# A fused attention and feed-forward kernel: score halves in separate banks, dummies at fixed places, one read moved, a new order for the first batch

## The chip, the cores and the metric

The kernel runs on one core of a Trainium2 chip. The metric is device time in microseconds (us); less is better. Five engines matter: PE (TensorE: matmuls, with its weight loads shown as PEld), DVE (VectorE), ACT (ScalarE), POOL (GpSimd) and SP (SyncE, which here issues most DMA transfers). Each engine works through its own list in order, and engines wait for each other through semaphores. SBUF is the working memory, PSUM the matmul output memory with eight banks of 128 x 512 float32, HBM the main memory.

## The reference

A two-way attention between tokens and a small state, for 8 batches with 8 heads, 512 tokens, 32 states and head width 64, then a two-layer network over all 8 x 544 rows:

```python
scores = x @ state.T / sqrt(D)          # per batch and head, 512 x 32
xread  = softmax(scores, over states) @ state
sread  = softmax(scores.T, over tokens) @ x
y = concat([xread, sread], rows)        # rows of all heads side by side: 4352 x 512
h = y @ w_in                            # 512 x 2048, given as float64
g = where(h >= 1, h, where(h <= -1, 0, (h + 1) ** 2 / 4))
out = g @ w_out                         # 2048 x 512, given as float64
```

## The kernel before

Stages run by batch (`b` = 0 to 7), and the 8 x 32 state rows come last as a ninth stage of half length. A batch has eight steps `j`, one for each 256 of the 2048 hidden columns.

The first attention product and the first layer are folded together: instead of `xread @ w_in` the kernel forms `sw` = state times the chunk of `w_in` (`sw_product`, L374), and the hidden block is `h` = softmax weights times `sw` (`Hidden.product`, L437). To keep float32 accuracy with a fast matmul format, operands are split into a high and a low part (`ath`/`atl`, `swh`/`swl`, `gh`/`gl`, `woh`/`wol`), and a product is three matmuls (L451 to L453 and L527 to L529). The activation is `relu` and `square` on ACT and `bound` on DVE; then `gh` (`high`, L480) and `gl` (`low`, L487). `g2` (L505) adds the output product, 24 matmuls of 512 columns for a step; it runs one step behind.

The weights arrive as float64 and are made float32 on the chip: `fetch` (L558) reads 1 MB per chunk, `low` (L564) and `high` (L577) convert the two halves of each number, `join` (L583) puts them together. On the orders below these are `dma.i.c`, `low.i.c`, `high.i.c`, `w.c` for chunk c of `w_in`, and `dma.o.c`, `low.o.c`, `high.o.c`, `join.c`, `woh.c`, `wol.c` for `w_out`. The tile for a chunk of `w_in` has two buffers, so the third chunk's read waits for the first chunk's join.

Batch 0 has all of this at once: weights, scores, softmax and products. Its order on each engine is written out in `SEQ` (L22 to L27), and `Plan` (L31) only works out from planned costs in which order the steps are emitted, and, in `emit` (L88), how many short dummy matmuls (`warm`, L162) fill the planned gaps on PE. Steps of the attention are `sc` (scores), `turn` (transposition of the scores), `top1`, `less1`, `exp1`, `sum1`, `inv1`, `norm1`, `back` (softmax over states); `park` (L285) copies batch 0's scores aside for the later softmax over tokens (`top2`, `exp2`, `turn_blocks`, `shuffle`), whose weighted sum is `read2` (L327) with `scale2` and `place2` behind it. Batch 0's scores come in two halves (`sc.0.0`, `sc.0.1`), both written into one tile of two banks (`ps_mm`, one buffer). Other PSUM tiles are `ps_acc` (four banks) and `ps_h` (two banks). Engines that touch the same tile's bank take turns.

From batch 1 on the order is that of the loop at L870. At step 0 of a batch, between the two halves of the last output product, stand `read2` of that batch, four groups of `sw` products and the next batch's scores; `later` (L814) hangs further steps of the attention at the middle (`mid`) or end of a step. Batch 0's second softmax is hung in batch 1 (L852 to L854), its `read2` stands behind that of batch 2 (L880), and the `place2` of batches 0, 1 and 2 together at step 1 of batch 2 (L848). `place2` issues 16 small transfers on SP, `shuffle` 16 as well.

Of the kernel before, what the change touches and what calls it, by code (L numbers as in the profile page):

```python
# [104 lines left out]
def state_exchange_moe(  # L105
# [56 lines left out]
    def warm(n):  # L162

        for _ in range(n):
            nc.tensor.matmul(warmed[:, :P], lhsT=ident, rhs=ident, start=True, stop=True)  # L165
# [37 lines left out]
    class Attention:  # L203
# [9 lines left out]
        def scores(self, half=None):  # L213
            b = self.b
            if half != 1:
                sc = self.both = ps_mm(f"sc{b}")
# [4 lines left out]
            for pr in range(NPR):
                for hh in range(2):
                    rows = slice(hh * 64, hh * 64 + 64)
                    o = self.sc[hh][pr * NS:(pr + 1) * NS]
# [3 lines left out]
                    nc.tensor.matmul(o, lhsT=sb[rows, b, pr], rhs=m, start=True, stop=True)  # L228

# [3 lines left out]
        def turn(self, q, half=None):  # L233
            t = self.tokens(half)
            nc.vector.transpose(out=self.z[:, q, t], in_=self.sc[q][:, t])  # L235
# [49 lines left out]
        def park(self):  # L285
            self.e2 = srT.rearrange("p a b n -> p (a b n)").rearrange("p (q t) -> p q t", q=2)
            nc.scalar.copy(out=self.e2, in_=self.both)
            self.seen = [self.e2[:, q] for q in range(2)]

        def top2(self, q):  # L290
            b = self.b
# [7 lines left out]
            nc.vector.tensor_reduce(out=nm, in_=self.seen[q], op=ALU.max, axis=AX.X, negate=True)  # L299
            nc.vector.tensor_scalar_mul(nm, nm, SCALE)  # L300

        def exp2(self, q):
            nc.scalar.activation(
                out=self.e2[:, q], in_=self.seen[q], func=AF.Exp, bias=self.nm2[:, q:q + 1],
                scale=SCALE, accum_out=self.sum2[:, q:q + 1],
# [258 lines left out]
    def low(kind, c, engine):  # L564
# [7 lines left out]
        else:  # L572
            nc.scalar.activation(
                out=lo, in_=lo.bitcast(U32), func=AF.Relu, scale=0.875 * 2.0 ** -29, bias=offset
# [369 lines left out]
```

## Time and profile before

| | us |
|---|---|
| median of 3 runs | 643.0 |
| lowest and highest | 642.75, 643.68 |
| profiled execution | 644.25 |
| its span, first to last instruction | 642.4 |
| 512-column matmul, from start to start | 0.227 |
| DVE STREAM_TRANSPOSE of 128x512 (L275), ACT COPY of the scores (L287) | 0.68, 1.01 |

The page lists busy time of each engine and groups of instructions, the timeline lists single instructions with the wait ahead of them in brackets and what ended it, and busy time can be asked for any stretch. A timeline row reads: start, duration, engine, line, operation, output and inputs, shape, count, and in brackets the idle time before it with its releaser. A row of a stretch reads: its length, then busy time and number of instructions (x) of PE, PEld, DVE, ACT and POOL, then the granted clock, the share of the DMA engines and GB/s. A matmul's own duration is longer than the distance between two, since they overlap. A row of a waits view reads: total, times, longest.

### The profile page before, as it was taken

How to read it: one execution, taken by the hardware profiler on the slowest of the kernel's cores; microseconds unless marked ns; L12 is line 12 of the kernel's file. 1: busy time of each engine (PE TensorE's matmuls, PEld its weight loads, DVE VectorE, ACT ScalarE, POOL GpSimd, SP SyncE). 2: the span in 40 equal slices, each digit the busy share in tenths (PEclk: the TensorE clock that was granted, in tenths of full speed). 3: DMA queues.
4: the chain of work that ended last, by engine and by line, in shares of the span. 5: the costliest groups of instructions: out<-in, count | busy, mean ns of one | idle time of the engine just before them, and what ended most of it. 6: DMA issues, size and time to landing. Idle time of an engine off the chain costs nothing.

```text
span 642.4 us, 10553 instructions
## 1 busy us (share of the span) xinstructions
PE 630.6 (98%) x4348; PEld 512.7 (80%) x4348; DVE 361.0 (56%) x539; ACT 370.7 (58%) x536; POOL 0.8 (0%) x7
## 2 busy tenths in 40 slices
PE   6999999999999999999999999999999999999997
PEld 5677787888788887888788887888788878888896
DVE  5999966555455536654565536653565534335431
ACT  5999865565555555555655556555755555444641
POOL 0000000000000000000000000000000000000000
PEclk9999999999999999999999999999999999999999
DMA  7996033123303301121212212011202110000101
GB/s 313 383 407 240 1 62 104 66 34 44 124 7 82 87 25 52 62 34 65 69 68 30 69 53 85 9 26 65 71 2 33 66 67 5 1 0 1 66 1 33
DMA packets 52191, 48.40 MB, mean 75 GB/s; under 512 B 42288, under 2 KB 42416, under 8 KB 49200
## 3 DMA queue, kind: packets, MB, share of 16 engines
q1 hardware_dynamic: 51808, 47.40, 22.9%
q8 instruction: 34, 0.56, 0.4%
q10 hardware_dynamic: 336, 0.33, 0.2%
q14 instruction: 13, 0.11, 0.1%
HBM read 34.08 MB, written 8.91 MB: 67 GB/s over the span
## 4 chain that ended last, share of the span: by engine, by line
PE 92%; DVE 4%; ACT 2%; DMA 1%; issue 1%; POOL 0%; ACTq 0%; POOLq 0%
PE acc L528 18%; PE acc L529 18%; PE acc L527 18%; PE h L451 10%; PE h L452 10%; PE h L453 10%; PE sw L386 4%; PE sr L337 1%; PE sc L228 1%; DMA raw_i<-in_moe_w_in_dram 1%; ACT raw_i L581 1%; DVE w L593 1%; PE warmed L165 1%; DVE u L475 0%; DVE z L235 0%
## 5 line engine op out<-in xcount | busy, mean ns | idle before, releaser
L529 PE MATMUL acc<-wo,gl 128*128 128x512 f32 x544 | 211.9, 389 | 0.1
L528 PE MATMUL acc<-wo,gh 128*128 128x512 f32 x544 | 211.7, 389 | 0.0
L527 PE MATMUL acc<-wo,gh 128*128 128x512 f32 x544 | 211.7, 389 | 0.0
L468 ACT ACTIVATE u<-h,half 128x512 f32<-128x512 f32 x136 | 93.3, 690 | 168.0 <-PE h L453 165.4
L475 DVE SCALAR_TENSOR_TENSOR u<-u,h 128x512 f32<-128x512 f32 x136 | 92.7, 686 | 167.7 <-ACT u L472 167.6
L489 DVE TENSOR_TENSOR gl<-u,gh 128x1024 fp32r<-128x1024 f32 x68 | 83.3, 1225 | 74.8 <-ACT gh L626 74.6
L529 PEld LDWEIGHTS acc<-wo,gl 128*128 128x128 f32 x544 | 102.1, 188 | 21.9 <-DVE gl L489 0.8
L528 PEld LDWEIGHTS acc<-wo,gh 128*128 128x128 f32 x544 | 102.1, 188 | 21.1
L527 PEld LDWEIGHTS acc<-wo,gh 128*128 128x128 f32 x544 | 102.1, 188 | 21.1
L626 ACT CAST gh<-u 128x1024 fp32r<-128x1024 f32 x66 | 69.3, 1050 | 40.6 <-DVE u L475 40.3
L472 ACT ACTIVATE u<-u 128x512 f32<-128x512 f32 (+1 forms) x128 | 84.4, 660 | 4.1
L386 PE MATMUL sw<-w,sb 64*32 64x256 f32 x1024 | 34.1, 379 | 3.7 <-DVE w L593 3.1
L386 PEld LDWEIGHTS sw<-w,sb 64*32 64x32 f32 x1024 | 20.3, 106 | 14.5 <-DVE w L593 4.0
L542 ACT COPY o<-acc 128x512 f32<-128x512 f32 x33 | 19.1, 587 | 15.3 <-PE acc L529 15.3
L451 PE MATMUL h<-ath,sw_3h 128*128 128x512 f32 x64 | 25.3, 395 | 0.8 <-DVE u L475 0.8
L452 PE MATMUL h<-ath,sw_3l 128*128 128x512 f32 x64 | 24.9, 390 | 0.0
L453 PE MATMUL h<-atl,sw_3h 128*128 128x512 f32 x64 | 24.9, 389 | 0.0
L451 PE MATMUL h<-ath,sw_1h 128*128 128x512 f32 x60 | 24.3, 405 | 0.0
L452 PE MATMUL h<-ath,sw_1l 128*128 128x512 f32 x60 | 23.5, 391 | 0.0
L453 PE MATMUL h<-atl,sw_1h 128*128 128x512 f32 x60 | 23.4, 390 | 0.0
L451 PE MATMUL h<-ath,sw_5hl 128*128 128x512 f32 x56 | 21.8, 389 | 0.0
L452 PE MATMUL h<-ath,sw_5hl 128*128 128x512 f32 x56 | 21.8, 389 | 0.0
(175 smaller groups left out, 715.0 us busy)
## 6 DMA issues: line engine op xcount, KB each, us to landing
xt<-in_xt_dram SPq DMA_DIRECT2D x16, 512.0 KB, 4.6
raw_i<-in_moe_w_in_dram SPq DMA_DIRECT2D x8, 1024.0 KB, 6.7
raw_o<-in_moe_w_out_dram SPq DMA_DIRECT2D x8, 1024.0 KB, 10.3
out_dram<-o SPq DMA_DIRECT2D x32, 256.0 KB, 2.1
xn<-in_x_dram SPq DMA_DIRECT2D x7, 1024.0 KB, 4.8
e<-eb SPq DMA_DIRECT2D x112, 32.0 KB, 2.0
srT<-rt SPq DMA_DIRECT2D x128, 4.0 KB, 1.7
xn<-in_x_dram SPq DMA_DIRECT2D x2, 512.0 KB, 4.5
```

What stands on the lines that cost most here:

```text
L386: nc.tensor.matmul(banks[hh][pr * NS:(pr + 1) * NS, i * CI:(i + 1) * CI], lhsT=sb[rows, bi, pr], rhs=w32[ci][rows, pr], start=True, stop=True,
L451: nc.tensor.matmul(o, lhsT=wh[:, k, sl], rhs=ah[:, k], start=first, stop=False)
L452: nc.tensor.matmul(o, lhsT=wl[:, k, sl], rhs=ah[:, k], start=False, stop=False)
L453: nc.tensor.matmul(o, lhsT=wh[:, k, sl], rhs=al[:, k], start=False, stop=last)
L468: nc.scalar.activation(out=self.u[:, i], in_=self.hs[i], func=AF.Relu, scale=0.5, bias=half)
L472: nc.scalar.activation(out=u, in_=u, func=AF.Square)
L475: nc.vector.scalar_tensor_tensor(out=self.u[:, i], in0=self.u[:, i], scalar=1.0, in1=self.hs[i], op0=ALU.min, op1=ALU.max,)
L489: nc.vector.tensor_tensor(out=gl, in0=self.u, in1=gh.bitcast(F32), op=ALU.subtract)
L527: nc.tensor.matmul(a, lhsT=lh, rhs=oh, start=f == 0, stop=False)
L528: nc.tensor.matmul(a, lhsT=lh, rhs=ol, start=False, stop=False)
L529: nc.tensor.matmul(a, lhsT=ll, rhs=oh, start=False, stop=f == NF - 1)
L626: nc.scalar.copy(out=out, in_=src)
```

## The change

Scores: the second half of batch 0's scores goes to two `ps_h` banks instead of the other columns of the first tile, and `park` becomes two steps of two copies each. Dummies: `warm` makes one matmul of 512 columns instead of 128; two at the start instead of seven, and four ahead of `sw.0.0` and one ahead of `p.0.0.0` by a table (`FILL`), none by planned gaps. Batch 0's second softmax moves to batch 1's step 1, and its `read2` and `scale2` to step 5, `place2` to step 6; batch 1's `place2` moves to step 4 of batch 2. Batch 7's last `sw` group takes the `ps_mm` tile instead of two `ps_acc` banks. The ACT form of `low` has another scale and no bias tile. The order lists of batch 0 change.

```diff
-WARM = 7
+WARM = 2
+FILL = {"sw.0.0": 4, "p.0.0.0": 1}
-            if self.engine[k] == "PE":
-                if begun[first] < begun[k] < begun[until]:
-                    n = int((begun[k] - idle) / 0.34)
-                    if n > 0:
-                        fill(n)
-                idle = done[k]
+            fill(FILL.get(k, 0))
             self.ops[k][2]()
...
-            nc.tensor.matmul(warmed[:, :P], lhsT=ident, rhs=ident, start=True, stop=True)
+            nc.tensor.matmul(
+                warmed.rearrange("p (a c) -> p a c", c=P), lhsT=ident, rhs=ident[:, None].broadcast_to([P, 4, P]),
+                start=True, stop=True,
+            )
...
-                sc = self.both = ps_mm(f"sc{b}")
-                self.sc = [sc[:, hh] for hh in range(2)]
+                sc = ps_mm(f"sc{b}")
+                self.sc = [[sc[:, hh]] for hh in range(2)]
...
+            else:
+                for hh in range(2):
+                    self.sc[hh].append(ps_h(f"sc{b}_{hh}"))
...
-        def park(self):
-            self.e2 = srT.rearrange("p a b n -> p (a b n)").rearrange("p (q t) -> p q t", q=2)
-            nc.scalar.copy(out=self.e2, in_=self.both)
-            self.seen = [self.e2[:, q] for q in range(2)]
+        def park(self, half):
+            if half == 0:
+                self.e2 = srT.rearrange("p a b n -> p (a b n)").rearrange("p (q t) -> p q t", q=2)
+            for q in range(2):
+                nc.scalar.copy(out=self.e2[:, q, self.tokens(half)], in_=self.seen(q, half))
...
-                out=lo, in_=lo.bitcast(U32), func=AF.Relu, scale=0.875 * 2.0 ** -29, bias=offset
+                out=lo, in_=lo.bitcast(U32), func=AF.Relu, scale=0.9375 * (2.0 ** -29 - 2.0 ** -49)
...
+    def one(b, *names):
+        for name in names:
+            f, *q = name.split()
+            getattr(atts[b], f)(*map(int, q))
+
+    later("mid", 1, 1, (one, 0, "top2 0", "exp2 0", "top2 1", "exp2 1"))
+    later("end", 1, 1, (one, 0, "turn_blocks 0", "turn_blocks 1", "shuffle"))
     later("end", 1, 2, (load_later, 0))
-    later("mid", 1, 4, *[(f, q) for q in range(2) for f in (lambda q: atts[0].top2(q), lambda q: atts[0].exp2(q))])
-    later("end", 1, 5, *[(lambda q: atts[0].turn_blocks(q), q) for q in range(2)], (lambda: atts[0].shuffle(),))
+    later("mid", 1, 5, (one, 0, "read2", "scale2"))
+    later("mid", 1, 6, (one, 0, "place2"))
+    later("mid", 2, 4, (one, 1, "place2"))
     for b in range(2, B):
-        later("mid", b, 1, (place_all, b))
+        later("mid", b, 1, (one, b, "place2"))
...
-                sr = atts[b].read2()
-                if b == 2:
-                    atts[0].read2(sr)
+                atts[b].read2()
...
-                sw_product([(b, 7), (b + 1, 0)][:B - b], ps_acc, "raw")
+                sw_product([(b, 7), (b + 1, 0)][:B - b], ps_acc if b + 1 < B else None, "raw")
```

The orders (`SEQ`) of batch 0 and the first steps of the next, broken into lines here, old (-) and new (+); a step is named with its batch and chunk or step, `p.i.0.j` is half i of hidden block j, `g2.i.0.j` half i of its output product:

```
-SP:
-    dma.xt.0.0 dma.xt.0.1 dma.i.0 dma.i.2 dma.o.0 dma.i.1 dma.o.1 dma.sb.1 dma.i.4 dma.i.3 dma.o.2 dma.xt.1
-    dma.o.4 dma.i.5 dma.i.6 dma.o.3 dma.o.5 dma.o.6 dma.xn.1 dma.i.7 dma.o.7 dma.xt.2 dma.eb.1
+SP:
+    dma.xt.0.0 dma.xt.0.1 dma.i.0 dma.i.2 dma.o.0 dma.i.1 dma.o.1 dma.o.2 dma.i.4 dma.i.3 dma.o.4 dma.o.3 dma.o.7
+    dma.sb.1 dma.i.5 dma.xt.1 dma.i.6 dma.o.6 dma.xt.2 dma.xn.1 dma.o.5 dma.i.7 dma.eb.1
-PE:
-    warm sc.0.0 sc.0.1 sw.0.0 p.0.0.0 p.1.0.0 sw.0.1 sw.0.2 p.0.0.1 p.1.0.1 g2.0.0.0 g2.1.0.0 p.0.0.2 sw.0.3
-    p.1.0.2 g2.1.0.1 sc.1 p.0.0.3 p.1.0.3 g2.0.0.1 g2.1.0.2 g2.0.0.2 p.0.0.4 sw.0.5 p.1.0.4 g2.0.0.3 g2.1.0.3
-    p.0.0.5 p.1.0.5 g2.1.0.4 sw.0.7 p.0.0.6 p.1.0.6 g2.1.0.5 g2.0.0.4 p.0.0.7 p.1.0.7 g2.0.0.5 g2.0.0.6 g2.1.0.6
+PE:
+    warm sc.0.0 sc.0.1 sw.0.0 p.0.0.0 p.1.0.0 sw.0.2 sw.0.1 p.0.0.1 p.1.0.1 g2.0.0.0 g2.1.0.0 p.0.0.2 sw.0.3
+    p.1.0.2 g2.1.0.1 g2.0.0.1 p.0.0.3 p.1.0.3 sc.1 g2.0.0.2 g2.1.0.2 p.0.0.4 p.1.0.4 g2.1.0.3 sw.0.5 g2.0.0.3
+    p.0.0.5 p.1.0.5 g2.0.0.4 g2.1.0.4 sw.0.7 p.0.0.6 p.1.0.6 g2.1.0.5 g2.0.0.5 p.0.0.7 p.1.0.7 g2.0.0.6 g2.1.0.6
-DVE:
-    turn.0.1.0 top1.0.1.0 turn.0.0.0 top1.0.0.0 turn.0.1.1 turn.0.0.1 top1.0.1.1 less1.0.1 top1.0.0.1 less1.0.0
-    w.0 sum1.0.0 inv1.0.0 sum1.0.1 norm1.0.0 inv1.0.1 back.0.0 norm1.0.1 back.0.1 w.2 ath.0.1 join.0 w.1 atl.0.1
-    atl.0.0 bound.1.0.0 swl.0.1 bound.0.0.0 wol.0 gl.0.0 low.o.1 low.i.3 swl.0.2 w.4 join.1 bound.0.0.1
-    bound.1.0.1 w.3 gh.0.1 wol.1 gl.0.1 swl.0.3 join.2 bound.0.0.2 woh.2 bound.1.0.2 wol.2 top2.1.0 turn.1.0
-    gl.0.2 low.i.5 top2.1.1 turn.1.1 w.5 w.6 join.3 top1.1.1 bound.0.0.3 bound.1.0.3 top1.1.0 wol.3 gl.0.3
...
+DVE:
+    turn.0.1.0 turn.0.0.0 turn.0.1.1 top1.0.1.0 turn.0.0.1 top1.0.0.0 top1.0.1.1 top1.0.0.1 less1.0.1 less1.0.0
+    w.0 sum1.0.0 sum1.0.1 inv1.0.0 norm1.0.0 inv1.0.1 back.0.0 norm1.0.1 back.0.1 w.2 low.i.1 atl.0.0 w.1 atl.0.1
+    join.0 bound.1.0.0 swl.0.1 bound.0.0.0 wol.0 gl.0.0 low.i.4 join.1 swl.0.2 w.4 low.i.3 bound.0.0.1 bound.1.0.1
+    w.3 wol.1 gl.0.1 join.2 low.o.7 swl.0.3 woh.2 wol.2 bound.1.0.2 bound.0.0.2 join.4 gl.0.2 join.3 turn.1.1
+    top2.1.0 woh.3 turn.1.0 bound.1.0.3 bound.0.0.3 top2.1.1 wol.3 top1.1.1 gl.0.3 w.6 w.5
...
-ACT:
-    park.0 low.i.0 high.i.0 exp1.0.0 low.i.2 exp1.0.1 high.i.2 swh.0.0 high.o.0 ath.0.0 low.o.0 high.i.1 low.i.1
-    relu.0.0.0 relu.1.0.0 square.0.0 swh.0.1 woh.0 swh.0.2 gh.0.0 high.i.4 low.i.4 relu.0.0.1 high.o.1 relu.1.0.1
-    square.0.1 high.i.3 low.o.2 woh.1 high.o.2 swh.0.3 relu.0.0.2 relu.1.0.2 square.0.2 low.o.4 high.i.5 low.i.6
-    gh.0.2 high.o.4 low.o.3 high.o.3 exp2.1.0 high.i.6 relu.0.0.3 relu.1.0.3 square.0.3 exp2.1.1 woh.3 high.o.5
-    gh.0.3 high.o.6 swh.0.5 relu.0.0.4 low.o.6 relu.1.0.4 square.0.4 woh.4 high.i.7 gh.0.4 low.i.7 exp1.1.0 woh.5
...
+ACT:
+    park.0.0 low.i.0 high.i.0 exp1.0.1 exp1.0.0 low.i.2 high.i.2 swh.0.0 park.0.1 low.o.0 ath.0.0 ath.0.1 high.i.1
+    high.o.0 relu.0.0.0 relu.1.0.0 square.0.0 swh.0.1 woh.0 swh.0.2 gh.0.0 high.o.1 low.o.1 high.i.4 relu.0.0.1
+    relu.1.0.1 square.0.1 high.i.3 woh.1 high.o.2 gh.0.1 low.o.2 relu.0.0.2 swh.0.3 relu.1.0.2 low.o.4 square.0.2
+    low.o.3 high.o.4 gh.0.2 high.o.3 low.i.5 high.i.5 relu.1.0.3 relu.0.0.3 square.0.3 low.i.6 exp2.1.0 low.o.6
+    gh.0.3 high.i.6 woh.4 relu.0.0.4 exp2.1.1 relu.1.0.4 square.0.4 high.o.7 swh.0.5 high.o.5 gh.0.4 low.o.5
+    high.i.7
...
```

More of the change, by code (lines that the diff above doesn't have):

```diff
@@ L86, in times, with emit @@
         self.begun, self.done = begun, done
-    def emit(self, fill, first, until):
+    def emit(self, fill):
         self.times()
-        begun, done = self.begun, self.done
-        idle = 0.0
         place = {k: i for seq in SEQ.values() for i, k in enumerate(seq.split())}
-        for k in sorted(begun, key=lambda k: (begun[k], place[k])):
-            if self.engine[k] == "PE":
-                if begun[first] < begun[k] < begun[until]:
-                    n = int((begun[k] - idle) / 0.34)
-                    if n > 0:
-                        fill(n)
-                idle = done[k]
+        for k in sorted(self.begun, key=lambda k: (self.begun[k], place[k])):
+            fill(FILL.get(k, 0))
             self.ops[k][2]()
@@ L157, in state_exchange_moe @@
     nc.vector.memset(half, 0.5)
-    offset = small.tile([P, 1], F32, name="offset")
-    nc.vector.memset(offset, 0.49)
     warmed = ps_acc("warmed")
@@ L223, in scores, with seen @@
                     rows = slice(hh * 64, hh * 64 + 64)
-                    o = self.sc[hh][pr * NS:(pr + 1) * NS]
+                    o = self.sc[hh][-1][pr * NS:(pr + 1) * NS]
                     m = self.xt[rows, :, pr]
                     if half is not None:
-                        o, m = o[:, half * S // 2:(half + 1) * S // 2], m[:, half]
+                        o, m = o[:, :S // 2], m[:, half]
                     nc.tensor.matmul(o, lhsT=sb[rows, b, pr], rhs=m, start=True, stop=True)
+        def seen(self, q, half=None):
+            return self.sc[q][0] if half is None else self.sc[q][half][:, :S // 2]
         def tokens(self, half):
@@ L233, in turn @@
         def turn(self, q, half=None):
-            t = self.tokens(half)
-            nc.vector.transpose(out=self.z[:, q, t], in_=self.sc[q][:, t])
+            nc.vector.transpose(out=self.z[:, q, self.tokens(half)], in_=self.seen(q, half))
         def parts(self, q):
@@ L298, in top2 @@
             nm = self.nm2[:, q:q + 1]
-            nc.vector.tensor_reduce(out=nm, in_=self.seen[q], op=ALU.max, axis=AX.X, negate=True)
+            src = self.seen(q) if b else self.e2[:, q]
+            nc.vector.tensor_reduce(out=nm, in_=src, op=ALU.max, axis=AX.X, negate=True)
             nc.vector.tensor_scalar_mul(nm, nm, SCALE)
@@ L303, in exp2 @@
             nc.scalar.activation(
[L304 to L305 removed]
+                out=self.e2[:, q], in_=self.seen(q) if self.b else self.e2[:, q], func=AF.Exp,
+                bias=self.nm2[:, q:q + 1], scale=SCALE, accum_out=self.sum2[:, q:q + 1],
             )
@@ L325, in shuffle, with read2 @@
                     )
-        def read2(self, sr=None):
+        def read2(self):
             b = self.b
             xn = loaded.pop(("xn", b))
-            c0 = 0 if sr is None else D
-            sr = ps_mm(f"sr{b}") if sr is None else sr
-            self.sr = sr[:, :, c0:c0 + D]
+            self.sr = ps_mm(f"sr{b}")[:, :, :D]
             for q in range(2):
@@ L340, in read2 @@
                         )
-            return sr
         def scale2(self):
@@ L675, in att_ops1 @@
                     h = k + (half,)
-                    op(("turn",) + h, "DVE", 0.35, m("turn", q, half), [("sc", b, half)], ends=[("sc", b)])
+                    op(("turn",) + h, "DVE", 0.35, m("turn", q, half), [("sc", b, half)],
+                       ends=[("sc", b, half), ("sch", b)][:1 + half])
                     op(("top1",) + h, "DVE", 0.35, m("top1", q, half), [("turn",) + h])
@@ L696, in att_ops2 @@
         if b == 0:
-            op(("park", b), "ACT", 0.95, m("park"), [("sc", b, 1)], ends=[("sc", b)])
+            for half in range(2):
+                op(("park", b, half), "ACT", 0.7, m("park", half), [("turn", b, q, half) for q in range(2)],
+                   ends=[("sc", b, half), ("sch", b)][:1 + half])
             return
@@ L702, in att_ops2 @@
             op(("top2",) + k, "DVE", 0.75, m("top2", q), [("sc", b)] + [("top2", b, 0)] * q, take=take)
-            op(("exp2",) + k, "ACT", 0.66, m("exp2", q), [("top2",) + k], ends=[("sc", b)])
+            op(("exp2",) + k, "ACT", 0.66, m("exp2", q), [("top2",) + k, ("turn",) + k], ends=[("sc", b)])
         for q in range(2):
@@ L788, in state_exchange_moe @@
         tensor(("sc", 0, side), 0.6, lambda side=side: att_start(0, side), [("dma", "xt", 0, side)],
-               take=[("mm", ("sc", 0))] * (1 - side), ends=[("xt", 0)])
+               take=[("mm", ("sc", 0, 0)), ("h", ("sc", 0, 1)), ("h", ("sch", 0))][side:1 + 2 * side], ends=[("xt", 0)])
     att_ops1(0)
@@ L884, in state_exchange_moe @@
                 sw_product([(b, 5), (b, 6)], ps_acc, "xn")
-                for c in (0, 2) if b == 2 else (b,):
-                    atts[c].scale2()
+                atts[b].scale2()
                 if b + 1 < B:
                     att_start(b + 1)
-                sw_product([(b, 7), (b + 1, 0)][:B - b], ps_acc, "raw")
+                sw_product([(b, 7), (b + 1, 0)][:B - b], ps_acc if b + 1 < B else None, "raw")
                 for c in (1, 3, 5, 7):
```

6 lines of the change are left out of this document (1 added, 5 removed), and 8 rows, old and new, of the table SEQ.

## The prediction

> **What bounds the kernel now.** First the busy times on the page, then busy time, clock and DMA by stretch (edges: the first matmul of batch 0's split products at 24.60 us, then the last matmul of each batch).
>
> ```profile
> PE 630.6 (98%) x4348; PEld 512.7 (80%) x4348; DVE 361.0 (56%) x539; ACT 370.7 (58%) x536; POOL 0.8 (0%) x7
> ```
>
> ```profile
> 0.00:24.60 24.60, 18.28 (x169) 13.42 (x169) 16.02 (x31) 16.72 (x22) 0.84 (x7) 1.00 0.83 326
> 24.60:96.67 72.07, 71.11 (x400) 55.04 (x400) 64.76 (x85) 61.71 (x74) 0.00 (x0) 1.00 0.54 203
> 96.67:168.32 71.65, 71.61 (x498) 57.98 (x496) 41.21 (x69) 40.69 (x64) 0.00 (x0) 1.00 0.28 74
> 168.32:241.42 73.10, 72.64 (x561) 58.93 (x560) 39.24 (x63) 39.41 (x60) 0.00 (x0) 1.00 0.20 54
> 241.42:312.43 71.01, 71.01 (x497) 57.85 (x496) 38.46 (x61) 39.32 (x60) 0.00 (x0) 1.00 0.19 54
> ```
>
> TensorE fills the span at a granted clock of 1.00, so only four places can give time: the start (24.6 us, whose real matmuls need about 7; 11.7 of its TensorE time are dummies), small waits in batch 0, and whatever batches 1, 2 and 7 have over a plain batch. A plain batch is 71.01; batch 1 has 0.64 more, batch 2 has 2.09 more. In batch 0 DVE and ACT are 90% and 86% busy, so there the order of their work counts.
>
> The start, by the timeline:
>
> ```profile
> 1.45 3.36 PE L165 MATMUL warmed<-ident 128*128 128x128 f32 x14 [1.45 <-POOL ident masks.py:199]
> 6.36 0.67 PE L228 MATMUL sc<-xt,sb 64*32 64x256 f32 x16 [0.62 <-DVE z L235]
> 6.96 3.62 PE L165 MATMUL warmed<-ident 128*128 128x128 f32 x30
> 8.52 1.25 ACT L573 ACTIVATE raw_i<-raw_i,offset 128x1024 int32<-128x1024 uint32 x1
> 8.66 0.78 DVE L235 STREAM_TRANSPOSE z<-sc 128x256 f32<-128x256 f32 x2 [0.62 <-ACT srT L287]
> 9.66 1.13 ACT L581 ACTIVATE raw_i<-raw_i 128x1024 f32<-128x1024 f32 x1
> 11.44 1.22 DVE L593 SCALAR_TENSOR_TENSOR w<-raw_i 128x1024 int32<-128x1024 int32 x1
> 12.69 0.33 SPq L561 DMA_DIRECT2D raw_i<-in_moe_w_in_dram  x1
> 12.71 0.67 PE L386 MATMUL sw<-w,sb 64*32 64x256 f32 x16 [2.14 <-DVE w L593]
> 16.26 3.67 PE L463 MATMUL h<-zt,sw_0w 128*128 128x512 f32 x8 [1.12 <-DVE zt L275]
> 19.08 1.19 ACT L581 ACTIVATE raw_i<-raw_i 128x1024 f32<-128x1024 f32 x1 [0.96 <-DMA raw_i<-in_moe_w_in_dram]
> 21.25 1.27 ACT L468 ACTIVATE u<-h,half 128x512 f32<-128x512 f32 x2
> 21.42 1.23 DVE L593 SCALAR_TENSOR_TENSOR w<-raw_i 128x1024 int32<-128x1024 int32 x1 [1.41 <-ACT raw_i L573]
> 26.88 1.23 DVE L489 TENSOR_TENSOR gl<-u,gh 128x1024 fp32r<-128x1024 f32 x1
> 28.16 0.50 PE L529 MATMUL acc<-wo,gl 128*128 128x512 f32 x1
> ```
>
> One chain: scores, softmax halves on DVE, chunk 0 joined (11.44), which frees the buffer for chunk 1's read (12.69, landed 18.99), chunk 1 split and joined (21.42), hidden block 0 on ACT and DVE, until its `gl` (26.88) lets the output product go on (28.16). The two waits of 0.62 are engines taking turns at one score tile.
>
> **The change part by part.**
>
> *Warm-up, 7 short dummies to 2 long.* 14 records in 3.36 are 0.24 each; the later ones, 30 in 3.62, are 0.12, so the first run at half rate. A 512-column record at full rate is 3.67/8 = 0.46, doubled and times 4: 3.4 to 3.7. I take nothing (bounds -0.1 and +0.3).
>
> *Second half of the scores in other banks, park in two.* Both 0.62 waits go. The next limit is chunk 0 itself, which landed at about 8.4:
>
> ```profile
> raw_i<-in_moe_w_in_dram SPq DMA_DIRECT2D x1, 1024.0 KB, 6.7
> raw_i<-in_moe_w_in_dram SPq DMA_DIRECT2D x1, 1024.0 KB, 6.3
> L568 DVE TENSOR_SCALAR raw_i<-raw_i x2: 686/689/692, 28.6 to 45.8; 128x1024 int32<-128x1024 uint32 x2
> ```
>
> (the issue at 1.68, the issue at 12.69, and the low word on DVE). DVE would be ready for the join at 10.3, but ACT's two passes end at 10.79 as before, so the join moves from 11.44 to 10.75: **-0.7**. Exps then follow at 10.65; the softmax steps keep their lengths, and `back` of both halves ends some 0.9 earlier, so the first products start near 15.3 for 16.26. The second park stands ahead of them, since its banks are theirs; it ends near 15.15 by the order on ACT: no wait, with 0.15 to spare.
>
> *Dummies before sw.0.0 and p.0.0.0.* 4 x 0.86 end near 10.1, 1 x 0.86 near 13.5: both in front of waits to 11.9 and 15.3. Nothing.
>
> *Chunk 1.* Its read moves 0.7 with the join; the same 6.3 gives 18.25. What is queued beside it is now o.2's 1 MB for sb's 448 KB (bounds 17.6 to 19.2). Its low word goes to DVE: 0.69 beside ACT's pass instead of after it, so its join stands at 19.5 for 21.42, and ACT, with two high passes left (2 x 1.04), reaches hidden block 0 at 20.4 for 21.25. DVE holds `atl` and the join of o.0 behind that landing; both are due only after 22. From there ACT's order is unchanged up to `gh` (relu, square, swh, woh, swh), so `gl` moves from 26.88 to 25.9 and the output product from 28.16 to 27.1: **-1.05**, bounds -1.8 and -0.2 with the landing.
>
> *The rest of batch 0's order.* ACT gets six steps from DVE and gives five: lows of o.1, i.5, o.5 (3 x 1.13 apart), two `gh` (0.95 each) and one `ath` (0.5) against four lows and one `woh`: +0.3 on ACT, -0.6 on DVE, so neither is relieved. What PE waits for now:
>
> ```profile
> 52.69 1.27 DVE L475 SCALAR_TENSOR_TENSOR u<-u,h 128x512 f32<-128x512 f32 x2
> 53.42 0.50 PE L451 MATMUL h<-ath,sw_3h 128*128 128x512 f32 x1 [0.82 <-DVE u L475]
> ```
>
> That is 1.2 between matmul starts, and 0.25 more in smaller waits. Followed step by step along the new lists with the durations above, chunk 3's join ends at 33.9 and holds sw.0.3 by 0.3; the bounds of block 2 end at 42.4, 0.5 late for block 3; the bounds of block 3, two low or high passes less in front of them on ACT, end before 51 and hold nothing; swl of chunk 5 costs 0.3. So 1.1 for 1.45: -0.35, batch 0 together **-1.4**. Bounds: all waits gone, -2.4; these three doubled and chunk 1 late, +0.5. On SP, xt.2 now waits for scores 1 (about 46), and i.7 for chunk 5's join (about 56.7), landing at 62 to 64; chunk 7 is wanted near 69.8: hidden by some 2 us.
>
> *Batch boundaries.*
>
> ```profile
> 98.02 3.22 PE L386 MATMUL sw<-w,sb 64*32 64x256 f32 x95
> 100.87 0.10 PEld L386 LDWEIGHTS sw<-w,sb 64*32 64x32 f32 x1 [0.52 <-issue]
> 168.63 1.10 PE L337 MATMUL sr<-xn,e 128*32 128x64 f32 x64
> 169.55 1.20 PE L337 MATMUL sr<-xn,srT 128*32 128x64 f32 x64
> 170.68 1.51 PE L386 MATMUL sw<-w,sb 64*32 64x256 f32 x43
> 172.64 1.22 PEld L386 LDWEIGHTS sw<-w,sb 64*32 64x32 f32 x51 [0.94 <-issue]
> 241.74 1.10 PE L337 MATMUL sr<-xn,e 128*32 128x64 f32 x64
> 242.77 2.82 PE L386 MATMUL sw<-w,sb 64*32 64x256 f32 x96
> 526.94 0.29 DVE L346 TENSOR_TENSOR rs<-sr,r 128x128 f32<-128x128 f32 x1 [0.99 <-PE sr L337]
> PEld sw L386 <- DVE sw_1l L413: 0.6, 2, 0.4
> L165 PE MATMUL warmed<-ident 128*128 128x128 f32 x80 | 11.7, 306 | 1.4 <-POOL ident masks.py:199 1.4
> q8 instruction: 34, 0.56, 0.4%
> ```
>
> Batch 2's 2.09 hold the second read (64 matmuls, 1.03) and 1.06 of idle put down to "issue". Moved into batch 1 the read costs 1.03 plus a change of shape on either side (241.74 to 242.77, and about 0.1 each): 1.25. Gain 0.85 if the idle goes. Queue q8 moved 34 packets for 2 x 4348 PE instructions: 256 each. I read the idle as PE outrunning such a packet: it comes where short matmuls use up 256 instructions fastest. An estimate from these rows, with 0.016 for a read (1.03/64), 0.029 for a sw (2.82/96): the 160 matmuls up to a packet's edge must last 4.2 to 4.6 us. Batch 1's edge at its 95th sw gives 0.23 + 64 x 0.016 + 95 x 0.029 = 4.0 (idle 0.6); batch 2's at its 43rd, 117 x 0.016 + 43 x 0.029 = 3.1 (idle 1.05); counting on, batches 3 to 6 have 4.8 or more, and none idles. The change drops 80 - 14 = 66 dummy records with their loads, half a packet: batch 1's edge falls among 0.23 us matmuls, **-0.6** (bounds -0.64 and +0.4). Batch 2's, counted on over 564 matmuls, then falls behind its sw: 51 x 0.016 + 96 x 0.029 + 13 x 0.054 (scores) = 4.3, idle 0.3 at most, which I take: **-0.5** (bounds -0.85 and +0.2). The Trainium skill ("Runtime: NRT & Kernel Launch", Instruction fetch mechanics) has the same 256 instructions in 16 KiB, but calls the refill mostly hidden; by that, the idle is something else and does not move with the count, which is a rival below.
>
> Batch 7's last chunk waits 0.6 for sw_1l to leave its banks; in the score tile, free once the read is scaled (526.94 + 0.29, two us earlier), it does not: **-0.5** (bounds -0.6, 0). The earlier steps of attention 0 (DVE 3.5 us in batch 1's step 1) lie in DVE's 42% of idle there; 16 DMAs instead of 48 at one place come off SP only.
>
> **Sum**: -1.4 - 0.6 - 0.5 - 0.5 = -3.0. The profiled execution took 644.25 (span 642.4): 641.25. The median of the runs is 643.0, and the same terms give **640.0**.
>
> **The rivals.**
>
> *The clock drops.* With fewer dummies TensorE works 1.3 of the 5 us between 18.75 and 23.8. For: the cold 0.24. Against: 2.14 idle at 12.71, at full rate after. If it drops, 12 matmuls take 0.43 for 0.23, 2.4 more, of which 0.5 lies in the wait for `gl`: +1.9, 641.9. The Trainium skill ("TensorE: Matmul & The Clock Gate", Why this matters for your kernels) wants no idle gap above about 3 us; no single gap here reaches that.
>
> *The idle at boundaries stays*, whatever the instruction count: batch 1 gives 0 and batch 2 costs +0.2: -1.4 - 0.5 + 0.2 = -1.7, 641.3. For: "issue" names no cause. Against: five batches without it.
>
> *Batch 0 gives nothing*: chunk 1's landing does not move, or the new lists wait on ACT twice as long as I find (its 86% speaks for that): -1.6, 641.4.
>
> *Slower: the edges land badly.* If my count is off by some 30 matmuls, packet edges sit in the reads of batches 3 to 7, where none idles now: 5 x 1.05 = +5.25 with -1.7 for the rest: 646.5. It turns slower once two of the five are hit at full price.
>
> **How the numbers follow.** Chances: forecast 0.55 (638.6 to 641.0), clock 0.12, idle stays 0.13, batch 0 nothing 0.14, edges 0.06. A measurement tells 0.2% (1.3 us) from none: faster means below 641.7. The forecast, both 641.3 cases for the most part and little of the clock's lie there: 0.81; same 0.13, slower 0.06. Range 638.6 to 641.9.
>
> **What would show it.** Right: second scores with no wait, chunk 0's join near 10.75, chunk 1's near 19.5, first `gl` product near 27.1; batch 1 about 72.3 (71.01 and the read), batch 2 about 71.3, no sw_1l wait in batch 7. Wrong: 512-column matmuls 0.43 apart after 23 us; "issue" at other boundaries; new waits on `u` or `w` between 33 and 62.

## The result and the profile after

| | us |
|---|---|
| before, median of 5 runs beside it | 643.68 (642.75 to 645.57) |
| after, median of 5 runs | 640.56 (640.12 to 641.01) |
| ratio, 95% interval | 0.9947 (0.9926 to 0.9968) |
| after, profiled execution and its span | 640.56, 638.8 |

The changed kernel is 3.1 us faster (643.68 - 640.56; 2.1 to 4.8 by the interval of the ratio), where 3.0 was forecast. The page of after, and its stretches by the same edges as before (first split product of batch 0 at 22.25, then the last 512-column matmul of each batch):

```profile
PE 627.1 (98%) x4282; PEld 505.7 (79%) x4282; DVE 359.6 (56%) x536; ACT 370.2 (58%) x539; POOL 0.8 (0%) x7
```

```profile
0.00:22.25 22.25, 15.23 (x102) 5.29 (x103) 15.66 (x30) 15.86 (x25) 0.83 (x7) 0.99 0.90 360
22.25:93.90 71.65, 71.65 (x400) 56.42 (x400) 63.90 (x84) 62.11 (x75) 0.00 (x0) 0.98 0.54 204
93.90:166.16 72.26, 72.26 (x562) 58.70 (x560) 41.86 (x71) 40.85 (x64) 0.00 (x0) 1.00 0.28 75
166.16:237.78 71.62, 71.62 (x497) 58.03 (x496) 38.52 (x61) 39.32 (x60) 0.00 (x0) 1.00 0.19 54
237.78:308.79 71.01, 71.01 (x497) 57.84 (x496) 38.45 (x61) 39.32 (x60) 0.00 (x0) 1.00 0.18 54
```

The end of batch 0 came from 96.67 to 93.90: -2.77, twice the forecast's -1.4. Batches 1 and 2 together took 143.88 (72.26 + 71.62) for 144.75 (71.65 + 73.10): -0.87, where -1.1 was forecast: batch 1 is as forecast (72.26, a plain batch and the read's 1.25), batch 2 kept 0.61 over a plain 71.01. The rest is equal to 0.01, batch 7 too. -2.77 - 0.87 is the span's -3.6; the medians differ by less, and the second profile of before, below, shows a likely reason.

The chain of the start in after, by the timeline:

```profile
5.89 0.67 PE L226 MATMUL sc<-xt,sb 64*32 64x256 f32 x16 [0.17 <-DMA xt<-in_xt_dram]
10.56 1.22 DVE L591 SCALAR_TENSOR_TENSOR w<-raw_i 128x1024 int32<-128x1024 int32 x1 [0.61 <-ACT raw_i L579]
11.81 0.33 SPq L559 DMA_DIRECT2D raw_i<-in_moe_w_in_dram  x1
15.16 3.67 PE L461 MATMUL h<-zt,sw_0w 128*128 128x512 f32 x8 [1.59 <-DVE zt L275]
16.91 1.20 ACT L579 ACTIVATE raw_i<-raw_i 128x1024 f32<-128x1024 f32 x1
18.55 1.22 DVE L591 SCALAR_TENSOR_TENSOR w<-raw_i 128x1024 int32<-128x1024 int32 x1
19.05 1.23 ACT L466 ACTIVATE u<-h,half 128x512 f32<-128x512 f32 x2
22.25 0.77 PE L449 MATMUL h<-ath,sw_1h 128*128 128x512 f32 x1 [1.76 <-DVE u L473]
24.53 1.22 DVE L487 TENSOR_TENSOR gl<-u,gh 128x1024 fp32r<-128x1024 f32 x1
26.99 0.39 PE L527 MATMUL acc<-wo,gl 128*128 128x512 f32 x1
170.76 0.10 PEld L226 LDWEIGHTS sc<-xt,sb 64*32 64x32 f32 x1 [0.49 <-issue]
526.90 0.50 PE L449 MATMUL h<-ath,sw_1h 128*128 128x512 f32 x1 [0.49 <-DVE sw_3l L411]
```

The waits of 0.62 on the score tile are gone, chunk 0 joins at 10.56 (forecast 10.75) and the first products start at 15.16 (15.3). Then chunk 1 runs ahead of the forecast: its read landed 5.0 after its issue, not 6.3, and its join is at 18.55, not 19.5. `gl` is ready 1.4 earlier than forecast, yet the first `gl` product starts at 26.99, almost the 27.1 of the forecast, because the clock fell in between (experiment 2 has the same order and no fall here, and starts it at 25.96):

```profile
20.00:22.00 2.00, 0.49 (x16) 0.01 (x2) 2.00 (x3) 1.97 (x5) 0.00 (x0) 0.99 1.02 418
22.00:24.00 2.00, 1.75 (x4) 1.55 (x5) 2.00 (x5) 1.88 (x3) 0.00 (x0) 0.50 0.98 414
24.00:26.00 2.00, 2.00 (x7) 1.52 (x7) 1.97 (x3) 2.00 (x3) 0.00 (x0) 0.65 1.05 438
```

The granted clock is the third number from the end. The last two rows of the chain belong to batches 2 and 7: 0.49 of "issue" idle stands behind the 13th of 16 scores, and the first hidden product of batch 7 waits for `sw_3l` where it used to wait for its chunk's turn.

### The profile page after: what moved, and what is told of

The parts are those of the page before. It is cut to its first block, busy times and chain, and to the rows that moved or that the text cites. A ratio compares the mean times of both kernels' runs of the same rounds, so it can differ in the third digit from the quotient of the medians.

```text
span 638.8 us, 10423 instructions
## 1 busy us (share of the span) xinstructions
PE 627.1 (98%) x4282; PEld 505.7 (79%) x4282; DVE 359.6 (56%) x536; ACT 370.2 (58%) x539; POOL 0.8 (0%) x7
## 4 chain that ended last, share of the span: by engine, by line
PE 95%; ACT 1%; DVE 1%; DMA 1%; issue 0%; SPq 0%; DVEq 0%
PE acc L525 19%; PE acc L526 19%; PE acc L527 19%; PE h L449 11%; PE h L450 10%; PE h L451 10%; PE sw L384 4%; PE sr L336 1%; DMA raw_i<-in_moe_w_in_dram 1%; PE sc L226 1%; DVE w L591 0%; ACT raw_i L571 0%; ACT raw_i L579 0%; DVE sw_1l L411 0%; DVE wf L591 0%; ACT raw_o L571 0%
## 5 line engine op out<-in xcount | busy, mean ns | idle before, releaser
L466 ACT ACTIVATE u<-h,half 128x512 f32<-128x512 f32 x136 | 93.3, 689 | 170.5 <-PE h L451 168.0
L624 ACT CAST gh<-u 128x1024 fp32r<-128x1024 f32 x68 | 71.4, 1050 | 41.7 <-DVE u L473 41.6
L384 PE MATMUL sw<-w,sb 64*32 64x256 f32 x1024 | 32.5, 378 | 2.1 <-DVE w L591 2.1
L540 ACT COPY o<-acc 128x512 f32<-128x512 f32 x33 | 19.1, 587 | 15.4 <-PE acc L527 15.3
```

Of the source, the lines that this page charges most:

```text
L384: nc.tensor.matmul(banks[hh][pr * NS:(pr + 1) * NS, i * CI:(i + 1) * CI], lhsT=sb[rows, bi, pr], rhs=w32[ci][rows, pr], start=True, stop=True,
L466: nc.scalar.activation(out=self.u[:, i], in_=self.hs[i], func=AF.Relu, scale=0.5, bias=half)
L624: nc.scalar.copy(out=out, in_=src)
```

## The experiments

Each was profiled once, beside the kernel before on the same chip, except the last, which was timed in five rounds. "Step" is the time from the last 512-column matmul of one batch to the first of the next: 5.82 in a plain batch, and in after 5.82, 6.44, 5.83, 5.82, 5.82, 5.82 and 5.09 in batches 1 to 7. "First read" is the first matmul of batch 1's `read2`, which shows what batch 0 gave: 94.22 in after.

**1. The kernel before, again.** No edit.

> The kernel before, once more, unchanged, for one question: how long i.1 takes from issue to landing. Theory A (its order of transfers makes it 6.3): 6.2 to 6.4 again, chunk 1's join near 21.4. Theory B (6.3 belongs to that one execution): 4.7 to 5.0 as in the five kernels profiled since, chunk 1's join near 20 and a total 0.5 to 1.4 under 644.25.

Total 643.5, span 641.7. The landing of chunk 1's read, then its join and batch 2's idle:

```profile
raw_i<-in_moe_w_in_dram SPq DMA_DIRECT2D x1, 1024.0 KB, 4.7
```

```profile
20.40 1.23 DVE L593 SCALAR_TENSOR_TENSOR w<-raw_i 128x1024 int32<-128x1024 int32 x1 [0.33 <-ACT raw_i L573]
171.90 1.23 PEld L386 LDWEIGHTS sw<-w,sb 64*32 64x32 f32 x51 [1.25 <-issue]
```

The same kernel, 1.6 less for the same read. Its join comes 1.0 earlier and its first read at 95.92 for 96.99. Theory B held for the mechanism: the 6.3 belonged to one execution. The total is 0.75 under 644.25, inside what was expected, and less than the 1.07 at the first read, since batch 2's idle was 1.25 for 0.94. The clock fell in this run too, to 0.50 from 12.7 to 16.1; from chunk 1's join to the first read it still took 75.52, for 75.57 without a fall. Against this profile the change gave -1.70 in batch 0 (95.92 to 94.22) and -1.18 up to batch 7: -2.9 in the span.

**2. The order of the transfers.** `dma.sb.1` directly behind `dma.o.1`, as before the change.

```diff
-dma.o.1 dma.o.2 dma.i.4 dma.i.3 dma.o.4 dma.o.3 dma.o.7 dma.sb.1
+dma.o.1 dma.sb.1 dma.o.2 dma.i.4 dma.i.3 dma.o.4 dma.o.3 dma.o.7
```

> Order of the transfers in batch 0: sb.1 is issued directly behind o.1 again, ahead of o.2, as in the kernel before. Theory A (how soon i.1 lands depends on which transfers are queued right behind it): i.1 takes 6.3 from issue to landing, not 5.0, chunk 1's join moves from 18.55 to about 19.9, and the first read of batch 1 comes about 1.3 later. Theory B (it depends on something else): i.1 takes 4.7 to 5.0 and nothing moves by over 0.2.

Total 640.15. i.1 took 4.7 again, first read 94.27. Theory B: what is queued behind a read did not set its landing. Experiment 3 issues it at 12.56, nearly before's 12.69, and it took 4.9: the time of issue doesn't either. Over the 14 profiles it was 4.6 to 5.0 in 13 and 6.3 in the one that the forecast was made from. Why that one was long stays open.

**3. Second score half back in the tile of the first.**

```diff
-                    self.sc[hh].append(ps_h(f"sc{b}_{hh}"))
+                    self.sc[hh].append(self.sc[hh][0][:, S // 2:])
```

> The changed kernel with the second half of batch 0's scores back in the first half's banks; all else as changed. Theory A (taking turns at the shared banks cost the start 0.7 to 0.9): the transpositions stand behind the second scores and the first park, chunk 0's join moves from 10.56 to 10.8 to 11.4, the first products from 15.16 to 15.4 to 16.0, and batch 1's first read by as much. Theory B (the order of DVE alone brought it, chunk 0's landing at 8.4 being the bound): join and products within 0.15.

Total 640.95. The wait is back, and everything behind it is later:

```profile
6.68 0.67 PE L226 MATMUL sc<-xt,sb 64*32 64x256 f32 x16 [0.94 <-DVE z L235]
11.31 1.22 DVE L591 SCALAR_TENSOR_TENSOR w<-raw_i 128x1024 int32<-128x1024 int32 x1
19.30 1.22 DVE L591 SCALAR_TENSOR_TENSOR w<-raw_i 128x1024 int32<-128x1024 int32 x1
```

Chunk 0's join moves by 0.75 (0.10 of it because its read landed at 8.43 for 8.33), chunk 1's by 0.75, the first read by 0.64 (94.86). This part of the change is worth 0.65, its forecast was 0.7.

**4. Low word of chunk 1 back on ACT.** `low.i.1` leaves DVE's list and stands behind `high.i.1` on ACT's.

> Low half of chunk 1 of batch 0 (low.i.1) goes back to ScalarE, behind the high half, as in the kernel before. Theory A (the chain of batch 0 is set by the order of these passes): chunk 1's join moves from 18.55 to about 19.2, the hidden block's relu from 19.05 to about 20.2, the gl product from 24.53 to about 25.6, and the first read of batch 1 comes 0.6 to 1.1 later than 94.22; total about 641.2 to 641.7. Theory B (another engine sets the pace behind it): the early steps move so, but the first read of batch 1 stays within 0.2 of 94.22; total about 640.6.

Total 642.88, more than either theory gave. DVE by the timeline, and the clock by stretch:

```profile
19.54 1.23 DVE L591 SCALAR_TENSOR_TENSOR w<-raw_i 128x1024 int32<-128x1024 int32 x1 [1.09 <-ACT raw_i L571]
25.97 1.23 DVE L487 TENSOR_TENSOR gl<-u,gh 128x1024 fp32r<-128x1024 f32 x1
```

```profile
22.00:24.00 2.00, 0.31 (x1) 0.34 (x2) 1.64 (x4) 2.00 (x4) 0.00 (x0) 0.74 1.02 406
24.00:26.00 2.00, 2.00 (x6) 1.58 (x6) 1.97 (x4) 1.90 (x4) 0.00 (x0) 0.50 1.01 410
26.00:28.00 2.00, 2.00 (x6) 1.61 (x5) 1.81 (x2) 2.00 (x2) 0.00 (x0) 0.50 0.99 414
28.00:30.00 2.00, 2.00 (x6) 1.52 (x6) 1.86 (x3) 2.00 (x4) 0.00 (x0) 0.55 1.01 426
```

The chain is as theory A has it: `gl` 25.97 for 24.53, 1.44 later (0.42 of it is already there at the first join). The first read is 2.79 later, at 97.01. The other 1.35 I put to the clock, at half rate for 6.8 us here against 3.4 in after. From the first split product to the first read the seven runs with the new order, the dummies and no fall there (experiments 2, 3, 5, 7, 10, 11 and 12) take 71.85 to 71.88; after and experiments 8 and 9, with a fall of 3.4, take 71.96, 72.14 and 72.14, and this run 73.32. No run has this edit without the fall, so that share is an inference.

**5. More dummies, ahead of hidden block 1.**

```diff
-FILL = {"sw.0.0": 4, "p.0.0.0": 1}
+FILL = {"sw.0.0": 4, "p.0.0.0": 1, "p.0.0.1": 2}
```

> The changed kernel with two more long dummies, right ahead of the split products of chunk 1 (p.0.0.1). In the changed kernel the clock was 0.50 from 22 to 24 us and 0.65 from 24 to 26, and the 12 matmuls of these products stood 0.43 apart. Theory A (TensorE stood nearly idle from 18.8 to 22.3, so its clock fell, and the slow matmuls are on the path): the clock stays 1.00, the matmuls stand 0.23 apart, the first product that needs gl comes near 25.8 for 27.0, and the first read of batch 1 starts 0.6 to 1.2 earlier than 94.22. Theory B (the clock falls but ACT and DVE set the pace behind it): matmuls 0.23 apart, but new waits on u or w between 27 and 45, and the first read of batch 1 within 0.2 of 94.22. If the fall has another cause than idleness, the clock falls again.

Total 640.36. The clock stays up:

```profile
22.00:24.00 2.00, 2.00 (x8) 1.24 (x7) 2.00 (x5) 1.85 (x4) 0.00 (x0) 1.00 1.00 422
```

and the first read is at 94.40, no earlier than with the fall. The time gained goes into waits on DVE further on, such as this one of PE by the waits view (total, times, longest), which after does not have:

```profile
PE h L450 <- DVE sw_5l L411: 0.2, 1, 0.2
```

Chunk 1's join came 0.27 later here than in after (18.82 for 18.55), so the two first reads alone hide its price. Counted from that join, the first read comes after 75.58 here and 75.55 to 75.58 in the six other runs without a fall there, after 75.66 in after, and after 75.84 and 75.83 in experiments 8 and 9: the fall of 3.4 us cost 0.1 in after and 0.3 in those two.

**6. No dummies.** `FILL = {}`.

> The five long dummy products at their set places are left out; the two ahead of the scores stay. Theory A (they keep the clock up): the granted clock falls earlier than 22, before the first h product, the hidden block's products of batch 0 run 0.43 apart for longer than 3 us and the first read of batch 1 comes 1 or more after 94.22. Theory B (they decide nothing, since the clock falls in some runs with them as well and VectorE and ScalarE set the pace): the first read of batch 1 stays within 0.3 of 94.22.

Total 641.17, first read 95.43. PE by the timeline and two stretches:

```profile
11.78 1.11 PE L384 MATMUL sw<-w,sb 64*32 64x256 f32 x16 [5.24 <-DVE w L591]
15.10 5.81 PE L461 MATMUL h<-zt,sw_0w 128*128 128x512 f32 x8 [2.21 <-DVE zt L275]
```

```profile
10.00:12.00 2.00, 0.22 (x8) 0.22 (x16) 1.63 (x3) 2.00 (x4) 0.00 (x0) 0.50 1.03 434
16.00:18.00 2.00, 2.00 (x4) 0.88 (x3) 2.00 (x4) 1.85 (x4) 0.00 (x0) 0.50 1.01 430
```

Theory A: here the fall, from 9.2 to 19.4, stands on the chain. The first products take 5.81 for 3.67, `relu` comes 1.04 later (20.09), the first read 1.21 later. The dummies are worth that much.

**7. Short dummies.** The four long ones become 16 of 128 columns: 48 instructions more ahead of everything.

```diff
-        for _ in range(n):
+        for _ in range(n if n != 4 else 16):
+            if n == 4:
+                nc.tensor.matmul(warmed[:, :P], lhsT=ident, rhs=ident, start=True, stop=True)
+                continue
```

> The changed kernel with the four long dummies ahead of sw.0.0 cut into sixteen short ones: the same TensorE time, 48 more instructions, so every packet edge of TensorE's instruction stream falls 24 matmuls earlier. Theory A (the idle at batch boundaries is TensorE outrunning a packet): batch 2's boundary (last product to first h) falls from 6.44 to 5.83, and the idle moves to batch 3 (5.83 to 6.3 or 6.6) and perhaps batch 4 (5.82 to 5.9 or 6.4); batches 1, 5, 6 keep 5.82. Theory B (the idle belongs to batch 2's own work): 6.44 stays in batch 2 and the others keep 5.82.

Total 640.0, first read 94.19. Batch 2's step is 5.82: its idle is gone, as theory A has it. But batches 3 and 4 have no idle (5.82 both), where A wanted some. Experiment 6, with 20 instructions less, has no idle in batch 2 either. The packet there took 1.47 us in experiment 6, longer than the 1.3 with which experiment 3 still idles by 0.34, so the place goes by the count. Whether the place costs something is another question, and kernels whose edge falls at the same score answer it. The packets of queue q8 in the 3.5 us from 167.5, 167.8, 168.1 and 168.0, in after, experiments 9, 3 and 8 (packets, MB, share of 16 engines):

```profile
q8 instruction: 1, 0.02, 2.9%
```

```profile
q8 instruction: 1, 0.02, 2.8%
```

```profile
q8 instruction: 1, 0.02, 2.3%
```

```profile
q8 instruction: 1, 0.02, 1.8%
```

A share of 2.9% is 0.029 x 3.5 x 16 = 1.6 us for one packet; then 1.6, 1.3 and 1.0. The steps of batch 2 are 6.44, 6.40, 6.16 and 5.89 in that order. Same instructions, same place, and the idle grows with the packet's time, from next to nothing at 1.0 us. (Experiments 2 and 4 have the same stream too, packets of 1.1 and 1.2, and steps of 5.86 and 5.85.) The idles at an edge, in all batches and kernels (0.2 to 1.25), end 1.15 to 1.4 after their packet has ended. In experiment 7 batch 2's packet took 1.9%, so the shift and a short packet both speak for its 5.82. Batch 3 idles by 0.23 in experiments 5, 8 and 9 (6.05): in 8 and 9 with packets of 1.75 and 1.67, where the same stream has none with 1.0 to 1.4 (after, experiments 2, 3 and 4). Experiment 5, with eight instructions more ahead of it, has it with a packet of 0.9; that one stays open.

**8. Last batch: splits of groups 1 and 3 in turns, bank by bank.**

```diff
+                if b + 1 == B:
+                    for q in range(2):
+                        for c in (1, 3):
+                            pt, wh, wl = sw_of[b, c][q]
+                            copy("ACT", wh, pt)
+                            nc.vector.tensor_tensor(out=wl, in0=pt, in1=wh.bitcast(F32), op=ALU.subtract)
-                for c in (1, 3, 5, 7):
+                for c in (1, 3, 5, 7)[2 * (b + 1 == B):]:
```

> The changed kernel; in batch 7 alone the splits of the groups of chunks 1 and 3 are interleaved bank by bank (1, 3, 1, 3 for 1, 1, 3, 3 on ACT and DVE). Theory A (the gain of the last chunk's new place was eaten by the next wait: the first h of step 1 needs a bank that chunk 3's group holds until its low part is out): that bank is free 0.6 earlier, batch 7's boundary (last product to first h) falls from 5.09 to 4.5 or 4.6, and the end comes 0.5 earlier. Theory B (something else holds the first h at 5.09): no change.

Total 640.33. Batch 7's step is 4.77 for 5.09, a gain of 0.32, less than expected:

```profile
526.70 0.50 PE L449 MATMUL h<-ath,sw_1h 128*128 128x512 f32 x1 [0.16 <-DVE sw_3l L897]
```

The wait for `sw_3l` fell from 0.49 to 0.16: it is what stood at the end of batch 7.

**9. The last chunk's place, undone alone.**

```diff
-                sw_product([(b, 7), (b + 1, 0)][:B - b], ps_acc if b + 1 < B else None, "raw")
+                sw_product([(b, 7), (b + 1, 0)][:B - b], ps_acc, "raw")
```

> Only the place of the last chunk in the last batch goes back, as before the change. Theory A (this edit alone is worth nothing, since the transposed weights of the third group come as late as those of the first): the step in batch 7 stays at 5.09, total as the changed kernel within 0.1. Theory B (it is worth what the prediction gave it): 5.6 in that step, total 0.5 longer.

Total 641.08; batch 7's step is 5.09 (last 512-column matmul 522.31, first product 527.40), as with the edit. Theory A: alone it is worth nothing. The 0.5 on the total lies elsewhere: first read 94.52, idle in batches 2 and 3 (6.40, 6.05).

**10. Batch 0's second read into batch 2.**

```diff
-    later("end", 1, 2, (load_later, 0))
-    later("mid", 1, 5, (one, 0, "read2", "scale2"))
-    later("mid", 1, 6, (one, 0, "place2"))
-    later("mid", 2, 4, (one, 1, "place2"))
-    for b in range(2, B):
+    later("end", 2, 2, (load_later, 0))
+    later("mid", 2, 5, (one, 0, "read2", "scale2"))
+    later("mid", 2, 6, (one, 0, "place2"), (one, 1, "place2"))
+    later("mid", 2, 7, (one, 2, "place2"))
+    for b in range(3, B):
```

> Batch 0's second read and its scaling move from batch 1 into batch 2. Theory A (the idle 0.49 ahead of a score in batch 2 belongs to a place in the instruction stream, which moves with the read): batch 1 loses the 1.25 insert, batch 2 gains it, the step from the last 512-wide product to the first h product in batch 2 is 5.82 plus the read's own 1.25 if it falls inside, with no idle behind a score; total 0.0 to 0.6 under that of the changed kernel. Theory B (the idle belongs to the work of batch 2's boundary): about 0.5 of idle again, total as the changed kernel.

Total 646.38: 5.8 lost. The theory on the idle held (steps of batches 1 and 2: 5.82 and 5.82), and the step of batch 3 became 10.88. SP, DVE and PE by the timeline:

```profile
211.77 21.06 SPq L354 DMA_DIRECT2D srT<-rt  x32
233.50 10.51 SPq L354 DMA_DIRECT2D srT<-rt  x16
245.25 0.31 DVE L348 STREAM_TRANSPOSE rt<-rs 128x128 f32<-128x128 f32 x1 [5.53 <-DMA srT<-rt]
246.20 2.25 PE L384 MATMUL sw<-w,sb 64*32 64x256 f32 x32 [3.19 <-DVE sw_1l L411]
```

I had moved 48 small copies to the end of batch 2. SP issues one in 0.66 (21.06/32), so the last 16, which read batch 2's tile `rt`, were issued until 244.0. Batch 3's rescale writes the same tile, so DVE stood 5.53, the splits behind it were late, and PE's last `sw` group waited 3.19 for its banks. That is 5.1 in the step. Another 1.0 lies behind it, where the clock fell after this wait, from 247.2 to 250.6:

```profile
248.00:251.00 3.00, 3.00 (x16) 2.12 (x8) 2.38 (x4) 1.07 (x2) 0.00 (x0) 0.57 0.07 12
```

The way from the first hidden product to the batch's last 512-column matmul took 66.22 there for 65.19 in after: in this stage nothing hides a fall. The kernel before also issued 48 such copies in a row, but from 171.5 to 202.8, early in batch 2, and no step shows a wait for them (batch 3: 5.82).

**11. The same read, other copies, and the turns of experiment 8.** Batch 2's and batch 1's copies ahead of the read, batch 0's in batch 3. Batch 0's weights lie where those copies go, so here part of these weights is overwritten before the read. The lines below are those of the read and the copies as they stand in this kernel, new ones with +.

```diff
+    later("end", 2, 2, (load_later, 0))
+    later("mid", 2, 5, (one, 0, "read2", "scale2"))
+    later("mid", 3, 4, (one, 0, "place2"))
     later("mid", 2, 4, (one, 1, "place2"))
```

> Two parts together: batch 0's second read in batch 2, with its 32 small copies to the states behind batch 2, in batch 3, so that never more than 32 stand in SyncE's queue ahead of batch 3's rescale; and the last batch's four splits of groups 1 and 3 in turns. Theory A (the 5.1 lost in the earlier move was the queue of those copies, and the idle of batch 2 goes with the read): the steps are 5.82 in batches 1 to 6 but for 0.3 at most, 4.8 in batch 7, 1.35 for the read in batch 2; span 0.6 to 1.0 under 638.8, total 639.5 to 640.0. Theory B (batch 3 stays late): over 6.5 in batch 3's step and no gain.

Total 650.86. Batch 3's step was down to 6.10, but PE waited at the read itself:

```profile
215.39 2.54 PE L336 MATMUL sr<-xn,srT 128*32 128x64 f32 x62 [8.56 <-DMA srT<-rt]
```

The read waits for batch 1's copies into the tile that it reads, issued only from 205.91 on. Batch 7's step was 4.76.

**12. The read first, then the copies, 16 to a stage more; and the turns.** Again the new lines alone.

```diff
+    later("end", 2, 2, (load_later, 0))
+    later("mid", 2, 5, (one, 0, "read2", "scale2"))
+    later("mid", 2, 6, (one, 2, "place2"))
+    later("mid", 3, 4, (one, 1, "place2"))
+    later("mid", 4, 4, (one, 0, "place2"))
+    for b in range(3, B):
```

> Batch 0's second read and rescale in batch 2, and only then the copies into the states, in three stages of 16 more each: batch 2's behind the read, batch 1's in batch 3, batch 0's in batch 4, since batch 0's weights for that read lie where the copies go; and the last batch's splits of groups 1 and 3 in turns. Theory A (what the two earlier moves lost was the queue of copies and the wait behind them, and the idle of batch 2 goes when the read leaves batch 1): steps of 5.82 in batches 1 to 6, at most one of them up to 0.3 longer, 1.35 for the read in batch 2, 4.8 in batch 7; span 637.9 to 638.4, total 639.4 to 640.0, 0.5 to 1.1 under the changed kernel's 640.56. Theory B (the read in batch 2 has a cost of its own): a step over 6.4 in batch 2 or 3, total 640.5 or more.

639.58 in five runs (639.48 to 639.76), ratio to before 0.9932 (0.9918 to 0.9946); span 637.8. Steps: 5.82, 5.82, 5.91, 5.82, 5.82, 5.82 and 4.77.

```profile
206.21 1.10 PE L336 MATMUL sr<-xn,srT 128*32 128x64 f32 x64
206.88 10.06 SPq L354 DMA_DIRECT2D srT<-rt  x16
525.94 0.50 PE L449 MATMUL h<-ath,sw_1h 128*128 128x512 f32 x1 [0.16 <-DVE sw_3l L898]
```

The read meets no wait, its copies are through before the rescale, and the span is 1.0 under after's: 0.62 from batch 2, 0.32 from batch 7. It is the fastest kernel of the study.

## Why the prediction was right, and which steps were not

The total came out as forecast, by the forecast mechanism in its largest parts. Against the second profile of before, batch 0 gave 0.3 more than forecast and batch 7 0.5 less. That these two nearly cancel, so that the total is within 0.1, is luck.

*The start* (-0.7): right. Experiment 3 measured 0.75 at the joins, 0.10 of it a later landing, and 0.64 at the end of batch 0.

*Chunk 1* (-1.05): the mechanism was right, the landing of its read was mis-sized. "The same 6.3" was taken from one row of one execution; it is 4.6 to 5.0 everywhere else (experiments 1 and 2). So 1.07 of the 2.77 in batch 0 is what that profile of before had too much, and the change itself gave 1.70 there, for 1.4. In after the read landed at 16.83, just before ACT was free for it (16.91).

*Dummies* ("nothing"): right as a cost, but they were not without effect: without them batch 0 ends 1.2 later (experiment 6). I had priced the dummies and not the clock that they hold.

*The clock drops* (rival, +1.9): it came where it was described, but over the first eight of the 12 matmuls (about 0.43 apart from 22.8 to 25.4), and its price was wrong: behind it other engines set the pace of batch 0, and the fall cost 0.1 in after and 0.3 in experiments 8 and 9 (experiment 5). Only `gl` had been taken as cover, and the cover was the rest of batch 0.

*The rest of batch 0's order* (-0.35): not tried by itself. Of the waits forecast at 0.3, 0.5 and 0.3, the profile of after has none, as PE came later; experiments 2 and 5, without a fall, have 0.2 at `sw_5l` and nothing at block 3. From the first split product to the first read it took 72.39 and 72.31 in the two profiles of before and 71.85 to 71.88 without a fall after: some 0.5 less, near the forecast. But the way from chunk 1's join to that product grew from 3.2 to 3.7, so from the join to the first read it is 75.57 and 75.52 before and 75.55 to 75.58 after. What batch 0 gained is what chunk 1's join gained; behind the join the new order as a whole saved nothing that these runs show.

*Batch 1* (-0.6): right; -0.62 by the steps (6.44 to 5.82).

*Batch 2* (-0.5): idle was expected behind the 13th score, 0.3 at most; it is there, at the 13th, and is 0.49. The count gave the place, but the size hangs on how long the packet takes (1.0 to 1.6 us, experiment 7), which no row of one execution can give. The rival that the idle does not follow the count fell with batch 1, where 0.62 went in every kernel with the new count, and with experiment 6; in experiments 7, 10 and 12 the packet was short (0.96 to 1.07), which could do it alone.

*Batch 7* (-0.5): failed. The last chunk no longer waits for its banks, as forecast, but the product behind it then waits for `sw_3l` (experiments 8 and 9), and the step is 5.09 as before. The trace of before had a row for the next wait, 0.4 on `sw_3l`; I did not ask what was late next.

*Edges land badly* (slower): none of batches 3 to 7 idled in after; elsewhere batch 3 did three times, by 0.23.

## What to carry to other kernels

Before a sum hangs on one transfer's or one packet's time, look for a second row of it: here one landing of 6.3, 4.7 in the next profile of the same kernel, was worth 1.07 us. Ask of every wait that is removed which one ends next, by name. A step that is moved takes its small transfers along: 48 copies of 0.66 us in one queue, late in a batch, cost 5.1 us and a fall of the clock 1.0 more; the same 48 early in a batch, and 16 to a stage, cost 0.1 at most.
